# One PSUM pool for attention and MLP, and a fixed order for the first MLP products

## The chip, the cores and the metric

The kernel runs on one core of a Trainium2 chip. The metric is the device time of one execution in microseconds (us): the time before is the median of three runs. Beside them stands one profiled execution, whose trace gives every instruction of the engines: PE (TensorE matmuls; PEld are its weight loads), DVE (VectorE), ACT (ScalarE), POOL (GpSimd) and SP, whose queue issues all DMAs here.

## The reference, cut to what matters

```python
def _attn_ref(q, k, v):                       # 8 batches, 12 heads, 448 positions, head size 64
    scores = scale * np.matmul(q, k.transpose(0, 1, 3, 2)) - np.log(S)
    attn = 1.0 / (1.0 + np.exp(-scores))      # a sigmoid, no row sums
    return np.matmul(attn, v)
x = attn_out.transpose(0, 2, 1, 3).reshape(B * S, H * D)      # 3584 tokens x 768
h = x @ w_in                                  # 768 x 2048 (float64 weights)
r = np.maximum(h, 0.0)
return ((r * r) @ w_out).astype(np.float32)   # 2048 x 768
```

## The kernel before, in words

The first phase is attention, 48 pairs of heads in turn (`step`, L302). For a pair, PE computes four blocks of scores, ACT takes the sigmoid of each into SBUF, and PE multiplies these by v into one PSUM bank, `pav` (L207). DVE copies that bank to `xo` (`put_x`, L219), and a DMA puts it into the scratch array `xd`. The two fp64 weight matrices are converted beside it.

The second phase is the MLP, four groups `g` of two batches. Each matrix product is done as seven products of half-size blocks (numbered 1 to 7, with sums and differences of blocks as operands), and every fp32 operand is split into a high part (`...h`, rounded by a cast) and a low part (`...l`, the remainder by a DVE subtraction), so that each block needs three matmuls: high x high, low x high, high x low. `gemm1` (L367) goes over eight chunks `i` of the hidden units; `run(n, i)` (L391) is product n of chunk i, nine matmuls with 448 columns each. It is called (n, i) below. Products 1, 6, 5 and 3 of a chunk accumulate one after the other in a bank "a", and ACT copies the value between them (`snap`, L387) or takes the ReLU; 7 and 4 go to a bank "b", and 2 to a bank "c". `gemm2` (L431) has three output chunks `e`; each product there is 24 matmuls for each e, and product 3 ends in `put("12", ...)`, an ACT copy out of bank "a" (L462), while product 4 adds to bank "b".

Each bank is a tile of its own from a PSUM pool. Attention has the pool `ps1` (L319): three tiles of two banks for scores, two of one bank for `pav`. The MLP has the pool `ps2` (L354), eight tiles of one bank. The second pool takes the memory of the first, so its first tile waits until the last tile of the first pool has been read.

The order on each engine is that of the code within `manual_schedule` (attention and the first operands of the MLP), and a list scheduler's own elsewhere; it can also slip its instructions between those of the written order. The engines run their queues strictly in order. At the end of attention `x_operands(0)` (L230) loads the attention output of the first two batches back from `xd` and returns eleven pieces: `make` splits a block (cast on ACT, L226; subtraction on DVE, L227), `sub` builds a difference (DVE, L244). The blocks x11, x21, x12, x22 are the operands of products 1, 2, 5 and 3; t1 to t4 are differences (t2 for product 6, t3 for 7, t1 for 5, t4 for 4). Before, the pieces and the weight splits `halve_weights` (L161; ACT cast L165, DVE subtraction L166) stand between the last attention steps, in the counts 1, 3, 3, and the rest after the last `put_x`. `first_44` is the first chunk's weights for products 1, 2, 6, 7, `first_45` those for 5, 3, 4. Weight tiles ("w") have eight buffers, so later weights wait on SP until the matmuls that read an earlier tile have ended. From `gemm2`, at product 3, `ahead` (L505) makes the next group's operands by the same pieces.

Of the kernel before, what the change touches and what calls it, by code (L numbers as in the profile page):

```python
# [41 lines left out]
PLACE = {n: i for i, n in enumerate(PRODUCTS)}  # L42
PH = 4
EARLY, LATE = slice(0, PH), slice(PH, 7)


@with_exitstack
def sigmoid_attention_relu2_mlp(
# [49 lines left out]
    def op1(name, dtype=F32):  # L98
        return sb.tile([P, S], dtype, tag="op1", bufs=N1, name=name)

    def wide(name, dtype=F32):
# [87 lines left out]

    def scores(ps, b, p, x):  # L190
        out = []
        for t in range(NT):
            sc = ps.tile([P, 2, 512], F32, tag="sc", bufs=3, name=f"sc_{b}_{p}_{t}")
            ks = slice(t * KT, (t + 1) * KT)
            for n, (kp, qp) in enumerate(((0, 0), (1, 0), (0, 1))):
                for j in range(2):
                    rows = slice(j * D, (j + 1) * D)
                    nc.tensor.matmul(  # L198
                        sc[:KT, j, :S], x[kp][rows, 1, ks], x[qp][rows, 0], start=(n == 0), stop=(n == 2)
                    )  # L200
            at = op2(f"at_{b}_{p}_{t}")
            nc.scalar.activation(at[:KT], sc[:KT, :, :S], AF.Sigmoid, bias=NEG_LOG_S, scale=SCALE)  # L202
            out.append(at)
        return out

    def attn_v(ps, b, p, at, vt):
        pav = ps.tile([P, 512], F32, tag="pav", bufs=2, name=f"pav_{b}_{p}")  # L207
        for t in range(NT):
            for j in range(2):
                nc.tensor.matmul(  # L210
                    pav[j * D : (j + 1) * D, :S],
                    vt[:KT, t, j * D : (j + 1) * D],
                    at[t][:KT, j],
                    start=(t == 0),
                    stop=(t == NT - 1),
                )
        return pav

    def put_x(b, p, pav):  # L219
        x = op1(f"xo_{b}_{p}")  # L220
        nc.vector.tensor_copy(out=x, in_=pav[:, :S])  # L221
        nc.sync.dma_start(out=xd[b, p], in_=x)

    def split(raw, name, new):
        hi, lo = new(name + "h", F32R), new(name + "l", F32R)
        nc.scalar.copy(out=hi, in_=raw)  # L226
        nc.vector.tensor_sub(out=lo, in0=raw, in1=hi.bitcast(F32))  # L227
        return hi, lo

    def x_operands(g):  # L230


# [14 lines left out]

        def make(product, n):
            (h2, l2), (h1, l1) = (split(r, f"{t}{n}_{g}", new) for r, t, new in zip(raw[n], "xy", (op2, op1)))
            ops[product] = [(h2[:, 0], l2[:, 0]), (h2[:, 1], l2[:, 1]), (h1, l1)]  # L250
# [6 lines left out]
        raw["t1"], raw["t3"], raw["t4"] = raw["12"], raw["11"], raw["21"]  # L257
        return ops, [
            lambda: make(1, "11"),
            lambda: make(2, "21"),  # L260
            lambda: sub("t1", "12", "11"),
            lambda: sub("t2", "22", "t1"),
            lambda: make(6, "t2"),
            lambda: sub("t3", "t2", "11"),
            lambda: make(7, "t3"),
            lambda: make(5, "t1"),
            lambda: make(3, "22"),
            lambda: sub("t4", "21", "t2"),
            lambda: make(4, "t4"),
        ]  # L270

# [29 lines left out]

    def step(ps, n):  # L302

        if n + XA <= last:
            x[n + XA] = load_pair(*pairs[n + XA])
        if n + VA <= last:
            vt[n + VA] = load_v(*pairs[n + VA])
        if n > 0:
            put_x(*pairs[n - 1], pav.pop(n - 1))
        if n + SA <= last:  # L310
            xs[n + SA] = split_pair(*pairs[n + SA], x[n + SA])
        if n < last:
            at[n + 1] = scores(ps, *pairs[n + 1], xs[n + 1])
        pav[n] = attn_v(ps, *pairs[n], at[n], vt[n])
        for k in range(NK):
            if k * NWP // NK == n:
                weights(k)

    with tc.tile_pool(name="ps1", bufs=2, space=PSUM) as ps:  # L319
        with tc.manual_schedule():  # L320
            wp = ps.tile([P, 2, 512], F32, tag="sc", bufs=3, name="warm_ps")
            for i in range(13):
                nc.tensor.matmul(wp[:, 0, :S], warm[:, :P], warm[:, :S], start=True, stop=True)
            x[0] = load_pair(*pairs[0])
            vt[0] = load_v(*pairs[0])
            x[1] = load_pair(*pairs[1])
            f64[0, 0] = load_chunk(*todo[0], 0)
            for n in (1, 2):
                x[n + 1] = load_pair(*pairs[n + 1])
                vt[n] = load_v(*pairs[n])  # L330
            f64[0, 1] = load_chunk(*todo[0], 1)
            for n in range(SA):
                xs[n] = split_pair(*pairs[n], x[n])
            at[0] = scores(ps, *pairs[0], xs[0])
            for n in range(last - 3):
                step(ps, n)
            ops[0], pieces = x_operands(0)
            first = {}
            for n, part, count in ((last - 3, EARLY, 1), (last - 2, LATE, 3), (last - 1, None, 3), (last, None, 0)):
                if part:  # L340
                    first[0, part == LATE] = load_weights(w1[0][:, part], f"first_{n}")
                step(ps, n)
# [12 lines left out]

    def bank(name):
        return ps.tile([P, 512], F32, tag="bank", bufs=8, name=name)[:, :S]

# [8 lines left out]
    def gemm1(g, ops, first):  # L367
# [23 lines left out]
        def run(n, i):  # L391
# [32 lines left out]

        for i in range(NI + 1):
            for n, j in ((1, i), (5, i - 1), (2, i), (6, i), (3, i - 1), (7, i), (4, i - 1)):
                if 0 <= j < NI:
                    run(n, j)
        return blocks

    def gemm2(g, blocks, ahead):  # L431
# [42 lines left out]
        for at, n in enumerate(order):  # L474
# [27 lines left out]
    for g in range(NG):  # L502
        blocks = gemm1(g, ops[g], {} if g else first)

        def ahead():  # L505
            if g + 1 < NG:
                ops[g + 1], pieces = x_operands(g + 1)
                for piece in pieces:
                    piece()

# [33 lines left out]
```

## Time and profile before

| | us |
|---|---|
| median of three runs (lowest, highest) | 1129.76 (1128.61, 1131.07) |
| the profiled execution | 1128.11 |
| its span, first to last instruction | 1126.3 |
| PE busy | 1109.9 (99%) |
| DVE busy | 779.0 (69%) |
| ACT busy | 614.4 (55%) |
| mean granted TensorE clock, as a share of full speed | 0.997 |

Busy time counts overlapping matmuls once. The rows of the trace give a start, a duration, the engine, the source line, the operation, out<-in with buffer and chunk numbers left out (so `w_1l` stands for several chunks, `x` for several blocks), and in brackets how long the engine sat idle before the row and what ended that. Matmuls overlap: the time that one takes in a row of them is the distance of their starts, not the duration shown; the same holds, by a little, for DVE and ACT.

### The profile page before, as it was taken

Reading aid. Unit: us, or ns where it says so; the run is one execution under the profiler, and the core shown is the slowest. Engines: PE = TensorE matmul, PEld = TensorE weight load, DVE = VectorE, ACT = ScalarE, POOL = GpSimd, SP = SyncE. Lnnn points to the kernel's source line nnn. Section 1 sums busy time; section 2 is a strip of 40 time slices with the busy share of each in tenths; the row PEclk is TensorE's granted clock in tenths of the full one; section 3 lists DMA queues with packets and bytes.
Section 4 is the critical chain, followed back from the end, with each engine's and each line's share of the span. In section 5 each row is a group of like instructions: output and inputs, shape, how many; then the busy total and the mean of one; then the engine's idle time right before and its main releaser. Section 6 shows DMA issues by size and latency. Waiting matters only on the chain.

```text
span 1126.3 us, 15056 instructions
## 1 busy us (share of the span) xinstructions
PE 1109.9 (99%) x5965; PEld 903.7 (80%) x5965; DVE 779.0 (69%) x869; ACT 614.4 (55%) x737; POOL 59.6 (5%) x36
## 2 busy tenths in 40 slices
PE   9999999999699999999999999999999999999998
PEld 4555455455499999999999999999999999999998
DVE  6778797877845589773557988454699745559951
ACT  6777787777634366553346466234556534346631
POOL 1122221221000000000000000000000000000000
PEclk9999999999899999999999999999999999999999
DMA  9989999999323333454324445333333652234431
GB/s 306 347 312 351 333 324 338 336 347 335 126 95 118 104 105 122 180 194 136 98 98 134 137 150 197 121 111 133 107 96 125 235 175 99 98 98 141 137 124 62
DMA packets 66503, 202.32 MB, mean 180 GB/s; under 512 B 6784, under 2 KB 33408, under 8 KB 66432
## 3 DMA queue, kind: packets, MB, share of 16 engines
q1 hardware_dynamic: 66432, 201.35, 52.4%
q8 instruction: 47, 0.77, 0.3%
q14 instruction: 24, 0.20, 0.1%
HBM read 157.29 MB, written 44.04 MB: 179 GB/s over the span
## 4 chain that ended last, share of the span: by engine, by line
PE 95%; DMA 2%; DVE 1%; ACT 1%; SPq 0%; issue 0%; ACTq 0%
PE ha L363 21%; PE oa L363 21%; PE pav L210 12%; PE hb L363 10%; PE ob L363 10%; PE sc L198 10%; PE hc L363 5%; PE oc L363 5%; DMA f<-w_in 1%; DMA first_45l<-w 1%; DMA w_1l<-w 0%; ACT at L202 0%; DVE xo L221 0%; DVE w_1l L166 0%; SPq L181 0%
## 5 line engine op out<-in xcount | busy, mean ns | idle before, releaser
L202 ACT ACTIVATE at<-sc 112x896 f32<-112x896 f32 x192 | 160.5, 925 | 69.2 <-PE sc L198 69.2
L166 DVE TENSOR_TENSOR w_1l<-w_1l,w_1h 128x1536 fp32r<-128x1536 f32 x59 | 103.5, 1755 | 87.2 <-ACT w_1h L165 87.2
L210 PE MATMUL pav<-at,v 112*64 112x448 f32 x768 | 154.9, 545 | 0.8 <-DVE xo L221 0.8
L389 ACT COPY s<-ha 128x448 f32<-128x448 f32 x96 | 51.1, 532 | 169.8 <-PE ha L363 147.7
L210 PEld LDWEIGHTS pav<-at,v 112*64 112x64 f32 x768 | 50.8, 136 | 83.7 <-issue 81.3
L165 ACT CAST w_1h<-w_1l 128x1536 fp32r<-128x1536 f32 x59 | 87.4, 1481 | 30.1 <-DMA w_1l<-w 29.7
L198 PE MATMUL sc<-qh 64*112 64x448 f32 x384 | 79.2, 408 | 2.5 <-ACT at L202 2.5
L198 PEld LDWEIGHTS sc<-qh 64*112 64x112 f32 x384 | 33.4, 170 | 51.1 <-issue 23.3
L422 DVE TENSOR_TENSOR g<-hb,s 128x448 f32<-128x448 f32 x32 | 20.0, 624 | 75.4 <-PE hb L363 75.4
L198 PE MATMUL sc<-qh,ql 64*112 64x448 f32 x384 | 70.8, 364 | 0.4 <-DVE ql L187 0.4
L165 ACT CAST w_0h<-w_0l 128x1536 fp32r<-128x1536 f32 x28 | 41.4, 1480 | 54.1 <-DMA w_0l<-w 54.1
L132 POOL TENSOR_TENSOR a<-a,f 128x768 int32<-128x768 int32 x32 | 59.4, 1857 | 212.3 <-DVE a L129 118.7
L198 PE MATMUL sc<-ql,qh 64*112 64x448 f32 x384 | 70.4, 362 | 0.0
L166 DVE TENSOR_TENSOR w_0l<-w_0l,w_0h 128x1536 fp32r<-128x1536 f32 x28 | 49.1, 1755 | 26.7 <-ACT w_0h L165 26.7
L221 DVE COPY xo<-pav 128x448 f32<-128x448 f32 x48 | 29.8, 622 | 50.4 <-PE pav L210 50.4
L165 ACT CAST w_5h<-w_5l 128x1152 fp32r<-128x1152 f32 x31 | 35.9, 1159 | 42.9 <-DMA w_5l<-w 28.2
L166 DVE TENSOR_TENSOR w_5l<-w_5l,w_5h 128x1152 fp32r<-128x1152 f32 x31 | 41.9, 1353 | 20.5 <-ACT w_5h L165 20.0
L187 DVE TENSOR_TENSOR ql<-x,qh 128x896 fp32r<-128x896 f32 x48 | 52.4, 1092 | 1.6
L385 DVE SCALAR_TENSOR_TENSOR g<-g 128x896 f32<-128x896 f32 x48 | 52.2, 1087 | 1.0
L186 DVE CAST qh<-x 128x896 fp32r<-128x896 f32 x48 | 41.0, 854 | 6.2 <-DMA x<-qk 6.2
L198 PEld LDWEIGHTS sc<-ql,qh 64*112 64x112 f32 x384 | 33.6, 171 | 5.5
L464 DVE TENSOR_TENSOR o<-ob,t 128x448 f32<-128x448 f32 x24 | 14.9, 620 | 32.9 <-PE ob L363 26.5
(597 smaller groups left out, 2961.4 us busy)
## 6 DMA issues: line engine op xcount, KB each, us to landing
w_1l<-w SPq DMA_DIRECT2D x59, 768.0 KB, 4.4
x<-qk SPq DMA_DIRECT2D x48, 448.0 KB, 7.3
w_0l<-w SPq DMA_DIRECT2D x28, 768.0 KB, 4.6
w_5l<-w SPq DMA_DIRECT2D x31, 576.0 KB, 4.2
f<-w_in SPq DMA_DIRECT2D x16, 768.0 KB, 6.8
w<-s SPq DMA_DIRECT2D x16, 768.0 KB, 3.8
f<-w_out SPq DMA_DIRECT2D x16, 768.0 KB, 6.3
v<-v SPq DMA_DIRECT2D x48, 224.0 KB, 7.3
```

The costliest lines, as they stand in the source:

```text
L132: nc.gpsimd.tensor_tensor(out=wb, in0=wb, in1=t.bitcast(I32)[:, :, 0], op=ALU.add)
L165: nc.scalar.copy(out=hi, in_=raw)
L166: nc.vector.tensor_sub(out=lo, in0=raw, in1=hi.bitcast(F32))
L186: nc.vector.tensor_copy(out=hi, in_=x)
L187: nc.vector.tensor_sub(out=lo, in0=x, in1=hi.bitcast(F32))
L198: nc.tensor.matmul(sc[:KT, j, :S], x[kp][rows, 1, ks], x[qp][rows, 0], start=(n == 0), stop=(n == 2))
L202: nc.scalar.activation(at[:KT], sc[:KT, :, :S], AF.Sigmoid, bias=NEG_LOG_S, scale=SCALE)
L210: nc.tensor.matmul(pav[j * D : (j + 1) * D, :S], vt[:KT, t, j * D : (j + 1) * D], at[t][:KT, j], start=(t == 0), stop=(t == NT - 1),)
L221: nc.vector.tensor_copy(out=x, in_=pav[:, :S])
L363: nc.tensor.matmul(out, a[:, c], b, start=first and n == 0, stop=last and n == 2, skip_group_check=True)
L385: nc.vector.scalar_tensor_tensor(out=t, in0=t, scalar=0.0, in1=t, op0=ALU.max, op1=ALU.mult)
L389: nc.scalar.copy(out=s, in_=banks["a", i])
```

## The change

There is one PSUM pool for the whole kernel: three tiles of two banks ("two") and two of one bank ("one"). In the MLP, banks "a" and "b" of a chunk are now the two halves of one "two" tile, which is taken at product 1; bank "c" is a "one" tile. The weights of the second chunk's products 1, 2, 6 and 7 (`w1_second`) are loaded within the written order, right behind `w1_late` (formerly `first_45`). The operands of products 1 and 2 are made by DVE alone, cast included: those of 1 behind the last step but two, those of 2 and the difference t1 behind the last step but one, t2 behind the last step. The last `put_x` follows, then the rest of the pieces with two of the weight splits among them. On PE, eleven products of group 0 get a fixed order relative to each other.

```diff
+FIRST_STEPS = ((1, 0), (2, 0), (1, 1), (2, 1), (6, 0), (7, 0), (6, 1), (5, 0), (7, 1), (3, 0), (4, 0))
+    ps = ctx.enter_context(tc.tile_pool(name="ps", bufs=2, space=PSUM))
+    def banks2(name):
+        return ps.tile([P, 2, 512], F32, tag="two", bufs=3, name=name)[:, :, :S]
+    def bank(name):
+        return ps.tile([P, 512], F32, tag="one", bufs=2, name=name)[:, :S]
...
+    def split(raw, name, new, vector=False):
         hi, lo = new(name + "h", F32R), new(name + "l", F32R)
-        nc.scalar.copy(out=hi, in_=raw)
+        if vector:
+            nc.vector.tensor_copy(out=hi, in_=raw)
+        else:
+            nc.scalar.copy(out=hi, in_=raw)
         nc.vector.tensor_sub(out=lo, in0=raw, in1=hi.bitcast(F32))
...
-            for n, part, count in ((last - 3, EARLY, 1), (last - 2, LATE, 3), (last - 1, None, 3), (last, None, 0)):
-                if part:
-                    first[0, part == LATE] = load_weights(w1[0][:, part], f"first_{n}")
-                step(ps, n)
-                if n == last - 2:
-                    halve_weights(first[0, False])
-                if n == last - 1:
-                    halve_weights(first[0, True])
-                for piece in pieces[:count]:
-                    piece()
-                del pieces[:count]
-            put_x(*pairs[last], pav[last])
-            for piece in pieces:
-                piece()
-    ps = ctx.enter_context(tc.tile_pool(name="ps2", bufs=8, space=PSUM))
+        first = {(0, False): load_weights(w1[0][:, EARLY], "w1_first")}
+        step(last - 3)
+        first[0, True] = load_weights(w1[0][:, LATE], "w1_late")
+        first[1, False] = load_weights(w1[1][:, EARLY], "w1_second")
+        step(last - 2)
+        pieces_of(1, vector=True)
+        halve_weights(first[0, False])
+        step(last - 1)
+        pieces_of(2, "t1", vector=True)
+        step(last)
+        pieces_of("t2")
+        put_x(*pairs[last], pav[last])
+        pieces_of(6)
+        halve_weights(first[1, False])
+        pieces_of("t3", 7)
+        halve_weights(first[0, True])
+        pieces_of(5, 3, "t4", 4)
...
-            if n in (1, 7, 2):
-                banks[k, i] = bank(f"h{k}_{g}_{i}")
+            if n == 1:
+                ab = banks2(f"h_{g}_{i}")
+                banks["a", i], banks["b", i] = ab[:, 0], ab[:, 1]
+            elif n == 2:
+                banks["c", i] = bank(f"hc_{g}_{i}")
...
+        if g == 0:
+            with tc.manual_schedule(engines={mybir.EngineType.PE}):
+                for n, i in FIRST_STEPS:
+                    run(n, i)
+            steps = [x for x in steps if x not in FIRST_STEPS]
...
-                if n in (1, 7, 2):
-                    banks[k, e] = bank(f"o{k}_{g}_{e}")
+                if n == 1:
+                    ab = banks2(f"o_{g}_{e}")
+                    banks["a", e], banks["b", e] = ab[:, 0], ab[:, 1]
+                elif n == 2:
+                    banks["c", e] = bank(f"oc_{g}_{e}")
```

The order on PE where the MLP begins: the first matmul of each piece of a product, before. In a name such as `ha_0_1` the numbers are the group and the chunk; `w1_0_1_1h` are the weights of chunk 1.

```order
L363 MATMUL ha_0_0_3264<-x11_0h_3073,first_44h_3009 128x448
...
L363 MATMUL hc_0_0_3276<-x21_0h_3138,first_44h_3009 128x448
...
L363 MATMUL hb_0_0_3299<-xt3_0h_3210,first_44h_3009 128x448
...
L363 MATMUL ha_0_1_3314<-x11_0h_3073,w1_0_1_1h_3309 128x448
...
L363 MATMUL ha_0_0_3264<-xt2_0h_3200,first_44h_3009 128x448
...
L363 MATMUL ha_0_1_3314<-x11_0l_3074,w1_0_1_1h_3309 128x448
```

The same place on PE of the changed kernel; the fifth to seventh rows are the first three matmuls of (1, 2).

```order
L378 MATMUL h_0_0_3267<-x11_0h_3131,w1_firsth_3009 128x448
...
L378 MATMUL hc_0_0_3279<-x21_0h_3189,w1_firsth_3009 128x448
...
L378 MATMUL h_0_1_3291<-x11_0h_3131,w1_secondh_3076 128x448
...
L378 MATMUL hc_0_1_3303<-x21_0h_3189,w1_secondh_3076 128x448
...
L378 MATMUL h_0_2_3396<-x11_0h_3131,w1_0_2_1h_3391 128x448
L378 MATMUL h_0_2_3396<-x11_0l_3132,w1_0_2_1h_3391 128x448
L378 MATMUL h_0_2_3396<-x11_0h_3131,w1_0_2_1l_3392 128x448
...
L378 MATMUL h_0_0_3267<-xt2_0h_3216,w1_firsth_3009 128x448
```

Product (1, 2), which is not among the eleven, stands between the fourth and the fifth of them, and needs the weights of chunk 2, high and low.

DVE behind the copy that the last `pav` product but one waits for, before (`xo_7_5` is the last copy of attention):

```order
L221 COPY xo_7_3_3150<-pav_7_3_3127 128x448
L166 TENSOR_TENSOR first_45l_3082<-first_45l_3082,first_45h_3081 128x1152
L227 TENSOR_TENSOR xt2_0l_3201<-xt_0_3007,xt2_0h_3200 128x896
L227 TENSOR_TENSOR yt2_0l_3205<-yt_0_3008,yt2_0h_3204 128x448
L244 TENSOR_TENSOR x11_0_2991<-xt_0_3007,x11_0_2991 128x896
L244 TENSOR_TENSOR y11_0_2992<-yt_0_3008,y11_0_2992 128x448
L166 TENSOR_TENSOR w1_0_1_1l_3310<-w1_0_1_1l_3310,w1_0_1_1h_3309 128x1536
L227 TENSOR_TENSOR xt3_0l_3211<-x11_0_2991,xt3_0h_3210 128x896
L227 TENSOR_TENSOR yt3_0l_3215<-y11_0_2992,yt3_0h_3214 128x448
L221 COPY xo_7_4_3218<-pav_7_4_3189 128x448
L221 COPY xo_7_5_3230<-pav_7_5_3221 128x448
```

DVE of the changed kernel from its last copy of attention; the second half of each pair (y, 448 wide) is left out from the third row on.

```order
L231 COPY xo_7_5_3213<-pav_7_5_3202 128x448
L240 TENSOR_TENSOR xt2_0l_3217<-xt_0_3007,xt2_0h_3216 128x896
L240 TENSOR_TENSOR yt2_0l_3221<-yt_0_3008,yt2_0h_3220 128x448
L176 TENSOR_TENSOR w1_secondl_3077<-w1_secondl_3077,w1_secondh_3076 128x1536
L258 TENSOR_TENSOR x11_0_2991<-xt_0_3007,x11_0_2991 128x896
...
L240 TENSOR_TENSOR xt3_0l_3229<-x11_0_2991,xt3_0h_3228 128x896
...
L176 TENSOR_TENSOR w1_latel_3074<-w1_latel_3074,w1_lateh_3073 128x1152
L240 TENSOR_TENSOR xt1_0l_3239<-x12_0_2995,xt1_0h_3238 128x896
...
L240 TENSOR_TENSOR x22_0l_3247<-x22_0_2999,x22_0h_3246 128x896
...
L258 TENSOR_TENSOR x21_0_3003<-x21_0_3003,xt_0_3007 128x896
...
L176 TENSOR_TENSOR w1_0_2_1l_3392<-w1_0_2_1l_3392,w1_0_2_1h_3391 128x1536
```

The copies have moved ahead of the MLP's operands, and the low part of chunk 2's weights is the last of what stands here.

PE in `gemm2` of group 0, the first matmuls of product 4 for e = 0, 1, 2 with the engines that they wait for, before:

```order
L363 MATMUL ob_0_0_4363<-o4_0_0h_4552,w2_0_4_0h_4571 128x448 [waits Activation_49]
L363 MATMUL ob_0_0_4363<-o4_0_0l_4553,w2_0_4_0h_4571 128x448
...
L363 MATMUL ob_0_1_4388<-o4_0_0h_4552,w2_0_4_0h_4571 128x448
L363 MATMUL ob_0_1_4388<-o4_0_0l_4553,w2_0_4_0h_4571 128x448
...
L363 MATMUL ob_0_2_4413<-o4_0_0h_4552,w2_0_4_0h_4571 128x448
```

And of the changed kernel, where bank "b" of chunk e is a half of the tile `o_0_e`:

```order
L378 MATMUL o_0_0_4021<-o4_0_0h_4540,w2_0_4_0h_4559 128x448 [waits Activation_49]
L378 MATMUL o_0_0_4021<-o4_0_0l_4541,w2_0_4_0h_4559 128x448
...
L378 MATMUL o_0_1_4048<-o4_0_0h_4540,w2_0_4_0h_4559 128x448 [waits Activation_49]
L378 MATMUL o_0_1_4048<-o4_0_0l_4541,w2_0_4_0h_4559 128x448
...
L378 MATMUL o_0_2_4075<-o4_0_0h_4540,w2_0_4_0h_4559 128x448 [waits Activation_49]
```

The matmuls for e = 1 and e = 2 now wait for ACT, which they did not before; for e = 0 the wait is there in both.

## Rows read from the trace of the kernel before

**Rows 1.** PE's waits: who for whom, total us, times, longest us.

```profile
PE ha L363 <- DVE xo L221: 8.2, 1, 8.2
```

**Rows 2.** Timeline of PE, last attention product and first MLP products.

```profile
290.14 3.23 PE L210 MATMUL pav<-at,v 112*64 112x448 f32 x16 [0.78 <-DVE xo L221]
...
301.53 0.74 PE L363 MATMUL ha<-x_0h,first_44h 128*128 128x448 f32 x1 [8.16 <-DVE xo L221]
...
304.96 0.37 PE L363 MATMUL hc<-x_0h,first_44h 128*128 128x448 f32 x1
...
306.82 0.37 PE L363 MATMUL hb<-xt_0h,first_44h 128*128 128x448 f32 x1
...
308.68 0.37 PE L363 MATMUL ha<-x_0h,w_1h 128*128 128x448 f32 x1
```

**Rows 3.** Windows: from:to, length, busy us (count) by engine, granted clock, DMA.

```profile
300.00:305.00 5.00, 3.47 (x10) 3.11 (x11) 5.00 (x8) 2.38 (x4) 0.00 (x0) 0.52 0.25 92
305.00:310.00 5.00, 5.00 (x26) 4.55 (x25) 4.82 (x6) 1.84 (x3) 0.00 (x0) 1.00 0.00 0
```

**Rows 4.** Timeline of DVE where attention ends.

```profile
289.47 0.61 DVE L221 COPY xo<-pav 128x448 f32<-128x448 f32 x1
290.01 1.34 DVE L166 TENSOR_TENSOR first_45l<-first_45l,first_45h 128x1152 fp32r<-128x1152 f32 x1
291.27 1.08 DVE L227 TENSOR_TENSOR xt_0l<-xt,xt_0h 128x896 fp32r<-128x896 f32 x1
292.27 0.61 DVE L227 TENSOR_TENSOR yt_0l<-yt,yt_0h 128x448 fp32r<-128x448 f32 x1
292.81 1.08 DVE L244 TENSOR_TENSOR x<-xt,x 128x896 f32<-128x896 f32 x1
...
297.12 1.76 DVE L166 TENSOR_TENSOR w_1l<-w_1l,w_1h 128x1536 fp32r<-128x1536 f32 x1 [2.69 <-ACT w_1h L165]
298.79 1.08 DVE L227 TENSOR_TENSOR xt_0l<-x,xt_0h 128x896 fp32r<-128x896 f32 x1
...
300.33 1.15 DVE L221 COPY xo<-pav 128x448 f32<-128x448 f32 x2
```

**Rows 5.** Timeline of ACT in the same stretch and behind it.

```profile
295.61 1.47 ACT L165 CAST w_1h<-w_1l 128x1536 fp32r<-128x1536 f32 x1 [5.16 <-DMA w_1l<-w]
296.99 0.93 ACT L226 CAST xt_0h<-x 128x896 fp32r<-128x896 f32 x1
297.83 0.56 ACT L226 CAST yt_0h<-y 128x448 fp32r<-128x448 f32 x1
...
315.10 1.15 ACT L165 CAST w_5h<-w_5l 128x1152 fp32r<-128x1152 f32 x1
```

**Rows 6.** Timeline of SP's DMA queue.

```profile
278.94 11.49 SPq L222 DMA_DIRECT2D xd<-xo  x2
290.52 0.88 SPq L158 DMA_DIRECT2D w_1l<-w  x2
...
311.39 0.32 SPq L158 DMA_DIRECT2D w_5l<-w  x1
```

**Rows 7.** The costliest group of DVE casts of this shape (page, part 5).

```profile
L186 DVE CAST qh<-x 128x896 fp32r<-128x896 f32 x48 | 41.0, 854 | 6.2 <-DMA x<-qk 6.2
```

**Rows 8.** Timelines: PE's first matmul of product 4, groups 0, 1, 2.

```profile
494.82 0.36 PE L363 MATMUL ob<-o_0h,w_0h 128*128 128x448 f32 x1
...
699.22 0.36 PE L363 MATMUL ob<-o_0h,w_0h 128*128 128x448 f32 x1
...
903.72 0.36 PE L363 MATMUL ob<-o_0h,w_0h 128*128 128x448 f32 x1
```

**Rows 9.** Timelines: ACT's three copies out of bank "a", groups 0, 1, 2.

```profile
495.93 1.58 ACT L462 COPY o<-oa 128x448 f32<-128x448 f32 x3
...
700.07 1.58 ACT L462 COPY o<-oa 128x448 f32<-128x448 f32 x3
...
904.99 1.58 ACT L462 COPY o<-oa 128x448 f32<-128x448 f32 x3
```

More of the change, by code (lines that the diff above doesn't have):

```diff
@@ L188, in split_pair, with scores @@
         return hi, lo
-    def scores(ps, b, p, x):
+    def scores(b, p, x):
         out = []
         for t in range(NT):
-            sc = ps.tile([P, 2, 512], F32, tag="sc", bufs=3, name=f"sc_{b}_{p}_{t}")
+            sc = banks2(f"sc_{b}_{p}_{t}")
             ks = slice(t * KT, (t + 1) * KT)
@@ L198, in scores, with attn_v @@
                     nc.tensor.matmul(
-                        sc[:KT, j, :S], x[kp][rows, 1, ks], x[qp][rows, 0], start=(n == 0), stop=(n == 2)
+                        sc[:KT, j], x[kp][rows, 1, ks], x[qp][rows, 0], start=(n == 0), stop=(n == 2)
                     )
             at = op2(f"at_{b}_{p}_{t}")
-            nc.scalar.activation(at[:KT], sc[:KT, :, :S], AF.Sigmoid, bias=NEG_LOG_S, scale=SCALE)
+            nc.scalar.activation(at[:KT], sc[:KT], AF.Sigmoid, bias=NEG_LOG_S, scale=SCALE)
             out.append(at)
         return out
-    def attn_v(ps, b, p, at, vt):
-        pav = ps.tile([P, 512], F32, tag="pav", bufs=2, name=f"pav_{b}_{p}")
+    def attn_v(b, p, at, vt):
+        pav = bank(f"pav_{b}_{p}")
         for t in range(NT):
@@ L210, in attn_v @@
                 nc.tensor.matmul(
-                    pav[j * D : (j + 1) * D, :S],
+                    pav[j * D : (j + 1) * D],
                     vt[:KT, t, j * D : (j + 1) * D],
@@ L220, in put_x @@
         x = op1(f"xo_{b}_{p}")
-        nc.vector.tensor_copy(out=x, in_=pav[:, :S])
+        nc.vector.tensor_copy(out=x, in_=pav)
         nc.sync.dma_start(out=xd[b, p], in_=x)
-    def split(raw, name, new):
+    def split(raw, name, new, vector=False):
         hi, lo = new(name + "h", F32R), new(name + "l", F32R)
-        nc.scalar.copy(out=hi, in_=raw)
+        if vector:
+            nc.vector.tensor_copy(out=hi, in_=raw)
+        else:
+            nc.scalar.copy(out=hi, in_=raw)
         nc.vector.tensor_sub(out=lo, in0=raw, in1=hi.bitcast(F32))
@@ L246, in x_operands, with make @@
         ops = {}
-        def make(product, n):
-            (h2, l2), (h1, l1) = (split(r, f"{t}{n}_{g}", new) for r, t, new in zip(raw[n], "xy", (op2, op1)))
+        def make(product, n, vector=False):
+            (h2, l2), (h1, l1) = (split(r, f"{t}{n}_{g}", new, vector) for r, t, new in zip(raw[n], "xy", (op2, op1)))
             ops[product] = [(h2[:, 0], l2[:, 0]), (h2[:, 1], l2[:, 1]), (h1, l1)]
@@ L300, in sigmoid_attention_relu2_mlp, with step @@
     NK = 3 * len(todo) + 1
-    def step(ps, n):
+    def step(n):
         if n + XA <= last:
@@ L312, in step @@
         if n < last:
-            at[n + 1] = scores(ps, *pairs[n + 1], xs[n + 1])
-        pav[n] = attn_v(ps, *pairs[n], at[n], vt[n])
+            at[n + 1] = scores(*pairs[n + 1], xs[n + 1])
+        pav[n] = attn_v(*pairs[n], at[n], vt[n])
         for k in range(NK):
@@ L354, in sigmoid_attention_relu2_mlp, with pieces_of @@
-    ps = ctx.enter_context(tc.tile_pool(name="ps2", bufs=8, space=PSUM))
-    def bank(name):
-        return ps.tile([P, 512], F32, tag="bank", bufs=8, name=name)[:, :S]
+    with tc.manual_schedule():
+        wp = banks2("warm_ps")
+        for i in range(13):
+            nc.tensor.matmul(wp[:, 0], warm[:, :P], warm[:, :S], start=True, stop=True)
+        x[0] = load_pair(*pairs[0])
+        vt[0] = load_v(*pairs[0])
+        x[1] = load_pair(*pairs[1])
+        f64[0, 0] = load_chunk(*todo[0], 0)
+        for n in (1, 2):
+            x[n + 1] = load_pair(*pairs[n + 1])
+            vt[n] = load_v(*pairs[n])
+        f64[0, 1] = load_chunk(*todo[0], 1)
+        for n in range(SA):
+            xs[n] = split_pair(*pairs[n], x[n])
+        at[0] = scores(*pairs[0], xs[0])
+        for n in range(last - 3):
+            step(n)
+        ops[0], pieces = x_operands(0)
+        first = {(0, False): load_weights(w1[0][:, EARLY], "w1_first")}
+        def pieces_of(*names, vector=False):
+            for name in names:
+                pieces[name](vector)
+        step(last - 3)
[14 more added lines that the diff above has]
+        pieces_of(5, 3, "t4", 4)
@@ L423, in run @@
                 squares("21", i)
[L425 to L428, printed above, removed]
+        steps = [
+            (n, j)
+            for i in range(NI + 1)
+            for n, j in ((1, i), (5, i - 1), (2, i), (6, i), (3, i - 1), (7, i), (4, i - 1))
+            if 0 <= j < NI
+        ]
+        if g == 0:
[3 more added lines that the diff above has]
+            steps = [x for x in steps if x not in FIRST_STEPS]
+        for n, i in steps:
+            run(n, i)
         return blocks
@@ L507, in ahead @@
                 ops[g + 1], pieces = x_operands(g + 1)
-                for piece in pieces:
-                    piece()
+                for piece in pieces.values():
+                    piece(False)
         gemm2(g, blocks, ahead)
```

46 lines of the change are left out of this document (13 added, 33 removed).

## The prediction

> **What bounds the kernel now.** I read the waits of TensorE first, since the page has PE busy for 99% of the span. The longest single wait by far is that of the first MLP matmul for DVE's last copies of attention [rows 1]. The timeline shows the place: the last attention product starts at 290.14 after 0.78 us of idle time for an earlier such copy, runs 3.23 us, and then PE is idle for 8.16 us, to 301.53 [rows 2]. The reader should see who ends the wait: two copies that start at 300.33 and take 1.15 us [rows 4], so to 301.48, and PE goes on 0.05 us later. That 0.05 is my price of a hand-over from here on. The copies were not late for want of data, since the product that they read had ended by 293.37; DVE worked through its written order, and one of its entries waited for a weight load (2.69 us idle at 297.12, whose cast on ACT had waited 5.16 us for the DMA) [rows 4, 5]. Behind the wait PE is slow: the first product's nine matmuls take from 301.53 to 304.96, 3.43 us, the third's from 306.82 to 308.68, 1.86 us, or 0.207 for one [rows 2]; the granted clock is 0.52 of full speed in 300 to 305 and 1.00 behind [rows 3], so the first nine ran at 1.2 GHz and the later ones at 2.4. The price of the whole transition is 0.78 + 8.16 + (3.43 - 1.86) = 10.5 us. Everywhere else in the MLP PE is gapless, so whatever makes it wait there is added to the time in full.
>
> **The change part by part.**
>
> *The pool wait goes.* A score tile is free long before 293, so the first MLP product no longer waits for the last copies. Their earlier place also frees the `pav` bank in time: the 0.78 goes. Attention then ends at 290.14 - 0.78 + 3.23 = 292.59, and PE goes straight on, if the operands of products 1 and 2 are there.
>
> *Products 1 and 2 by DVE.* Four casts come onto DVE. A 128x896 cast is 0.85 in the mean [rows 7]; the 448 wide one is not in the trace, at least 0, at most 0.85; I take 0.6, near the 448 wide subtraction (0.61). From starts in rows 4: a 448 copy 0.54, a pair of subtractions (896 and 448) 1.00 + 0.54 = 1.54, a 1152 split 1.26, a 1536 split 1.67. Before, three pairs stand between the first weights' split and the copy at 289.47, so that split was done by 289.47 - 4.62 = 284.85. Now come a copy, a split of x21 with its casts (1.54 + 1.45), t1 (1.54), a copy, t2 (1.54): 7.15 in all, to 292.0. The last copy has to wait for PE until 292.6 anyhow, so the casts cost nothing. That cover is 0.6 us; past it every microsecond delays the chain below by as much.
>
> *Four products run, then PE waits again.* (1,0), (2,0), (1,1) and (2,1) take 4 x 1.86 = 7.44, to 300.0. The next on PE is (1,2), which is not one of the eleven; its first two matmuls need the high part of chunk 2's weights, the third the low part. On DVE that low part is the last of what follows the last copy: 0.54 (copy) + 6 x 1.54 (t2 split, t3, t3 split, t1 split, x22 split, t4) + 1.67 + 1.26 + 1.76 (the three weight splits) = 14.47. DVE also waits for ACT's cast of t3: it starts 1.08 into the pair and takes 0.93 [rows 5], so 2.01 + 0.1 against 1.54, some 0.6. From 292.64 that is 307.7, and the third matmul can go at 307.8. The high part comes earlier: t3 is there at 292.64 + 0.54 + 1.54 + 1.67 + 1.08 = 297.5, and ACT then has three pairs of casts (0.84 + 0.56 each), the late weights (1.15) and this cast (1.47) [rows 5], to 304.3. So PE is idle from 300.0 to 307.8 but for two matmuls, 7.4 us, in place of 8.9: the wait has moved behind four products more than it has shrunk.
>
> *What that is worth.* I count matmuls done. The clock fell in the pause before; I take it that it falls in this one too, and that nine matmuls are slow again: 38 are done at 307.8 and 47 at 311.2. Before, 9 were done at 304.96 and 9 + 6.24 / 0.207 = 39 at 311.2. The gain is 8 x 0.207 = 1.6 us. From above: if the clock stays up, 1.57 more. From below: the load `w1_0_1_5` may start only when the first weights' last reader, now (7,0), has ended. Before it took from the issue at 311.39 to the end of the cast at 316.25 and 1.34 for the split, 6.2 us [rows 4 to 6]. Now 27 + 3 matmuls lie between (7,0) and the third of (5,1), 30 x 0.207 = 6.2; I take a wait of 0.3 (with a load as slow as the 5.1 us at 290.52, 1.4 more). The net gain is 1.3.
>
> *The loads.* The second chunk's weights went to DMA at 290.52, behind two copies that SP had waited 11.49 us to send [rows 6]; now they stand ahead of these, so at about 279, and are needed at 293. The third chunk's stand behind the last copies, so about 293.3; with the 5.1 us from issue to cast shown for both of 290.52 they are there by 298.4, needed at about 302.8. Neither costs anything.
>
> *Banks "a" and "b" in one tile.* In `gemm2`, product 4 adds to bank "b" while ACT still has to copy product 3's result out of "a". The order shows that the first matmul of product 4 now waits for ACT for e = 1 and 2, where before it did not: the tile is guarded as a whole. For e = 0 I read its old wait as the operand's and its new one as the later of operand and copy. In the trace product 4 starts at 494.82, 699.22 and 903.72 [rows 8], the three copies at 495.93, 700.07 and 904.99, each 1.58 / 3 = 0.53 [rows 9]. With the copy of e = 0 to wait for, PE stands 1.64, 1.38 and 1.80 us, with 0.05 each 4.97 in all. The copies of e = 1 and 2 end 1.05 later, behind one and two pieces of 24 matmuls (4.9 us each), and cost nothing. The fourth group makes no operands for a next one and its copies come promptly. ACT's queue ahead of the copies is the casts of the next group's operands, which are the same in both orders, and the transition shifts PE and them alike; so I take the whole 4.97. Bounds: 0, if the copies came as soon as product 3 ends, and 3 x 1.80 + 0.15 = 5.6.
>
> A rule of the Trainium skill speaks against this term. Its page PSUM — Partial Sum Buffer, section "PSUM bank collisions raise a hardware error", says that accesses have to be kept apart by bank (and quadrant), not more widely; the two halves are different banks. By that rule alone the sum would be without the 4.97. No run here shows the collision itself, but the wait stands in the program's order, whether the chip needs it or not.
>
> *The eleven products' order* otherwise costs nothing: a product is the same nine matmuls wherever it stands.
>
> **The sum.** 1128.11 (profiled execution) - 1.3 + 4.97 = 1131.8. The median of the runs lies 1.65 above that execution, so 1133.4.
>
> **Rivals.**
>
> *The four products bridge the gap* (faster). If what PE needs next were ready within 7.4 us of the end of attention, all 10.5 us would go, and with the 5.0 in `gemm2` the time would be 1129.76 - 10.5 + 5.0 = 1124.3. For it: DVE idled 2.69 us in this stretch [rows 4]. Against it: the chain is 14.5 us of plain DVE work.
>
> *The two halves cost no wait* (no change): the mechanism is a copy that is done before product 4 wants the bank, or the page's rule. 1129.76 - 1.3 = 1128.5. Against it: three groups out of three show the copy late by over 1.3 us.
>
> *The clock stays up in the new pause*, since two matmuls lie inside: 1133.4 - 1.57 = 1131.9. Against it: it had fallen in the one pause of this length that the trace has.
>
> *The transition gains nothing*: (5,1) waits 1.4 us more for its weights, or the casts overrun their cover. 1129.76 + 5.0 = 1134.8 and somewhat above.
>
> **Chances.** The forecast 0.60 (its own range 1132.2 to 1135.0), clock up 0.13, no gain 0.11, no wait in the halves 0.09, bridge 0.07. A measurement of this kernel tells 0.2%, 2.3 us, from no change; so slower begins at 1132.0. Slower: 0.57 of the forecast, the 0.11, and 0.05 of the clock's: 0.73. Same: the rest of these and the 0.09: 0.20. Faster 0.07. The range from 1130.8 to 1135.9 leaves out the bridge, most of the unwaited halves and a little above.
>
> **What would show it.** PE: the first MLP matmul right behind the last `pav`, about 292.6; a gap of some 7 us ahead of and in (1,2), ended by ACT's cast and DVE's split of chunk 2's weights; nine slow matmuls behind it; then a PE wait for ACT's copy of line 489 in three groups, 1.4 to 1.8 us each. It is wrong if (1,2) starts without a wait, if these three waits are missing, or if other waits of over 0.5 us on the halves of a tile appear in `gemm1`.

## The result and the profile after

The changed kernel took 1133.55 us (median of 11 runs, 1131.24 to 1135.40) against 1128.61 for the kernel before, timed beside it: a ratio of 1.0044, 95% interval 1.0029 to 1.0058, so some 5 us slower. The prediction was 1133.4, that is 3.6 us above the 1129.76 that it started from. The profiled execution took 1133.89 us, its span is 1132.1.

The waits of PE over the whole span of the changed kernel (engine and line, what ended the wait: us in total, times, the longest):

```profile
PE h L378 <- ACT w_1h L175: 3.9, 1, 3.9
PE o L378 <- ACT o L489: 3.7, 3, 1.6
...
PE h L378 <- DVE w_1l L176: 2.6, 1, 2.6
...
PE h L378 <- DVE g L431: 0.4, 1, 0.4
```

The 8.2 us of [rows 1] are gone. A wait of 3.9 and 2.6 us for the third chunk's weights stands in their place, three waits for ACT's copies are new, and so is one for an add of DVE (`g`, L431). PE's timeline shows the places (start, us, instruction, [idle before it <- releaser]):

```profile
292.73 0.47 PE L378 MATMUL h<-x_0h,w_firsth 128*128 128x448 f32 x1
...
300.00 0.37 PE L378 MATMUL hc<-y_0h,w_secondl 128*128 128x448 f32 x1
304.27 0.74 PE L378 MATMUL h<-x_0h,w_1h 128*128 128x448 f32 x1 [3.90 <-ACT w_1h L175]
304.81 0.57 PE L378 MATMUL h<-x_0l,w_1h 128*128 128x448 f32 x1
307.98 0.74 PE L378 MATMUL h<-x_0h,w_1l 128*128 128x448 f32 x1 [2.59 <-DVE w_1l L176]
308.51 0.57 PE L378 MATMUL h<-x_0h,w_1h 128*128 128x448 f32 x1
...
312.25 0.48 PE L378 MATMUL h<-xt_0l,w_firsth 128*128 128x448 f32 x1
312.57 0.36 PE L378 MATMUL h<-xt_0h,w_firstl 128*128 128x448 f32 x1
...
495.79 0.47 PE L378 MATMUL o<-o_0h,w_0h 128*128 128x448 f32 x1 [0.84 <-ACT o L489]
...
701.74 0.47 PE L378 MATMUL o<-o_0h,w_0h 128*128 128x448 f32 x1 [1.27 <-ACT o L489]
...
908.05 0.47 PE L378 MATMUL o<-o_0h,w_0h 128*128 128x448 f32 x1 [1.64 <-ACT o L489]
...
1002.46 0.47 PE L378 MATMUL h<-x_3h,w_5h 128*128 128x448 f32 x1 [0.42 <-DVE g L431]
```

The MLP starts at 292.73, right behind attention, where it was 301.53 [rows 2]. Four products later PE stops, does two matmuls, stops again, and from 308.51 to 312.25 a matmul takes 0.374 us. The windows say the same (us, busy us and instructions of each engine, granted clock, DMA):

```profile
295.00:300.00 5.00, 5.00 (x26) 4.55 (x25) 4.47 (x6) 2.23 (x3) 0.00 (x0) 1.00 0.47 157
300.00:305.00 5.00, 1.09 (x4) 0.50 (x2) 5.00 (x7) 4.22 (x6) 0.00 (x0) 0.73 0.00 0
305.00:310.00 5.00, 2.41 (x7) 1.83 (x6) 5.00 (x7) 2.27 (x4) 0.00 (x0) 0.50 0.02 3
310.00:315.00 5.00, 5.00 (x20) 4.33 (x19) 1.62 (x2) 0.53 (x1) 0.00 (x0) 0.75 0.00 0
```

A clock of 0.50 is the level of 1.2 GHz, as in [rows 3]. DVE is busy all through the pause. Its timeline has the last attention copy and the end of the chain to the third chunk's weights:

```profile
292.85 0.63 DVE L231 COPY xo<-pav 128x448 f32<-128x448 f32 x1 [0.68 <-PE pav L220]
...
306.17 1.75 DVE L176 TENSOR_TENSOR w_1l<-w_1l,w_1h 128x1536 fp32r<-128x1536 f32 x1
```

An account of PE's lost time: for each of the 4032 MLP matmuls of both traces I took by how much the interval between two starts exceeds the usual one (0.203 us, or 0.207 in stretches that the last section speaks of; I call this usual interval the pace). A wait comes out some 0.15 us longer this way than in PE's list, which counts from the shown end of the matmul before: 1.43 for the 1.27 at 701.74. Transition and `gemm1` of group 0: before 0.78 + 8.24 + 1.60 = 10.6, now 10.06, a gain of 0.55. `gemm2` of groups 0 to 2: 1.07 + 1.52 + 1.89 = 4.5 more. `gemm1` of group 3: 1.37 against 0.06, 1.3 more. Together 5.25; the spans differ by 5.8, of which 0.3 is a difference in pace and 0.2 lies in attention, from its start on. The executions of one kernel differ by up to 1%, and the pace alone is worth 11 us in one of the traces below, so the experiments are read by this account first and by their medians second. The ratio given with each run is against the kernel before, timed beside it. That kernel's own median there was 1130.75 (first four runs), 1130.83 (fifth to eighth) and 1129.70 (last two), against the 1128.61 beside the changed kernel, which was not timed again: a difference between a run's median and the changed kernel's 1133.55 is uncertain by some 2 us.

### The profile page after: what moved, and what is told of

Same layout as the page of the kernel before. It is cut to its first block, busy times and chain, and to the rows that moved or that the text cites. A ratio compares the mean times of both kernels' runs of the same rounds, so it can differ in the third digit from the quotient of the medians.

```text
span 1132.1 us, 15052 instructions
## 1 busy us (share of the span) xinstructions
PE 1113.6 (98%) x5965; PEld 903.8 (80%) x5965; DVE 782.7 (69%) x873; ACT 612.8 (54%) x733; POOL 59.8 (5%) x36
## 4 chain that ended last, share of the span: by engine, by line
PE 91%; DVE 3%; DMA 3%; ACT 2%; issue 1%; SPq 1%; ACTq 0%; DVEq 0%
PE h L378 30%; PE o L378 27%; PE pav L220 13%; PE sc L208 11%; PE oc L378 5%; PE hc L378 5%; DMA f<-w_in 1%; DMA w_0l<-w 1%; DMA w_1l<-w 1%; DVE w_1l L176 0%; DMA y<-xd 0%; DVE y L258 0%; ACT at L212 0%; ACT w_0h L175 0%; DVE x L258 0%
## 5 line engine op out<-in xcount | busy, mean ns | idle before, releaser
L404 ACT COPY s<-h 128x448 f32<-128x448 f32 x96 | 50.9, 533 | 164.9 <-PE h L378 141.2
L440 DVE TENSOR_TENSOR g<-h,s 128x448 f32<-128x448 f32 x32 | 20.0, 624 | 69.8 <-PE h L378 69.7
L378 PE MATMUL o<-o_0h,w_0h 128*128 128x448 f32 x144 | 52.3, 368 | 3.7 <-ACT o L489 3.7
L378 PE MATMUL o<-o_2h,w_1l 128*128 128x448 f32 x144 | 52.7, 366 | 0.0
L378 PE MATMUL o<-o_3l,w_1h 128*128 128x448 f32 x144 | 52.7, 366 | 0.0
```

The costliest lines, as they stand in the source:

```text
L378: nc.tensor.matmul(out, a[:, c], b, start=first and n == 0, stop=last and n == 2, skip_group_check=True)
L404: nc.scalar.copy(out=s, in_=banks["a", i])
L440: nc.vector.tensor_add(out=tile_of("21", i), in0=out, in1=snaps[2, i])
```

## The experiments

My theory was that two things decide: entries of DVE and ACT that stand in their queues ahead of what PE needs next, and the tile that guards banks "a" and "b" as one. Its rivals stand with each run.

**The pairing alone.** Before, with the halves of one tile in the second pool:

```diff
...
-            if n in (1, 7, 2):
-                banks[k, e] = bank(f"o{k}_{g}_{e}")
+            if n == 1:
+                ab = banks2(f"o_{g}_{e}")
+                banks["a", e], banks["b", e] = ab[:, 0], ab[:, 1]
+            elif n == 2:
+                banks["c", e] = bank(f"oc_{g}_{e}")
```

> The kernel before with one part of the change alone: in the MLP, banks a and b of one chunk are the two halves of one tile, in before's second pool (3 two-bank tiles, 2 one-bank tiles). The transition is as in before. Theory (the halves cost waits): in the changed kernel PE stood about 1.0, 1.4 and 1.8 us ahead of product 4 of gemm2 in the first three groups, and some 1.3 us more went in gemm1 of the last group; so this kernel is 4 to 5.5 us slower than before, and its trace shows a PE wait for ACT's copies of product 3's result, three times, that before does not have. Rival 1 (the copy is late only because the transition moved ACT's work): no such waits, within 1 us of before. Rival 2 (PE is slower for other reasons, a drift of the matmul pitch between two executions): no waits and yet some 2 us slower.

1134.01 us, ratio 1.0036 (1.0012 to 1.0059). The waits have both, the old one and the new:

```profile
PE h L366 <- DVE xo L221: 8.1, 1, 8.1
PE o L366 <- ACT o L468: 4.0, 3, 1.4
```

By the account `gemm2` loses 1.56, 1.53 and 1.65. So the pairing makes the three waits, with the old transition too. The second pool also has fewer tiles here than before's eight, but product 4 takes no new tile, so it is not their number that it waits for. `gemm1` of group 3 lost nothing (0.11): that part of the expectation missed.

**Fewer casts ahead of the copies.** The changed kernel, with the next group's operands made in two parts:

```diff
-            if n == 3:
-                ahead()
+            if n in (3, 4):
+                ahead(n)    # 3: operands of products 1 and 2; 4: the others
...
```

> The changed kernel, with one edit in gemm2: of the next group's operands only those of products 1 and 2 are made ahead of product 3, the others behind product 3, so that ACT comes to its copies of product 3's result with fewer casts in front. The tile pairing stays. Theory (it is the late copy, not the pairing by itself, that PE waits for): the three PE waits of 1.0, 1.4 and 1.8 us go, no new ones at the next group's start; 4.2 us faster than the changed kernel, some 0.5 us slower than before to 0.5 faster. Rival 1 (the pairing costs whatever ACT does, for instance because reading one bank holds up writes to its neighbour): no more than 1 us faster than the changed kernel. Rival 2 (the operands of products 6, 7 and on come late for the next group): new waits of 1 us or more in gemm1 of groups 1 to 3 take the gain back.

1125.64 us, ratio 0.998 (0.9949 to 1.001): no difference from before is clear of the noise. The profiled execution, at 1137.42, is the slowest of the twelve, by its pace (last section). No wait for ACT's copies is left in the list, and `gemm2` loses nothing in any group. The pairing costs only where the copy is late.

**Product (1,2) as the twelfth:**

```diff
-(6, 1), (5, 0), (7, 1), (3, 0), (4, 0))
+(6, 1), (5, 0), (7, 1), (3, 0), (4, 0), (1, 2))
```

> The changed kernel, with product (1,2) as the twelfth of the fixed order, so that it can no longer come between the fourth and the fifth. Theory of the prediction (PE waits for chunk 2's weights): with seven more products ahead of (1,2), 13 us, its weights are there in time, PE waits less than 2 us, and the kernel is 6 to 9 us faster than the changed one. Rival (the rest of the transition is as late: product (6,0) writes bank a, which ACT has first to copy, and this copy stands on ACT behind all casts of the transition): PE does four products and waits about as long as in the changed kernel, 6 to 8 us, now ahead of (6,0) and for ACT; within 1.5 us of the changed kernel. I think the rival likelier.

1134.17 us, 1.0026 (1.0006 to 1.0047), as the rival had it. PE's wait, and then ACT's timeline:

```profile
PE h L378 <- ACT s L404: 7.3, 1, 7.3
```

```profile
292.19 1.47 ACT L175 CAST w_secondh<-w_secondl 128x1536 fp32r<-128x1536 f32 x1
...
301.96 1.47 ACT L175 CAST w_1h<-w_1l 128x1536 fp32r<-128x1536 f32 x1
304.96 0.94 ACT L239 CAST xt_0h<-x 128x896 fp32r<-128x896 f32 x1 [1.53 <-DVE x L258]
305.80 0.56 ACT L239 CAST yt_0h<-y 128x448 fp32r<-128x448 f32 x1
306.27 0.96 ACT L404 COPY s<-h 128x448 f32<-128x448 f32 x2
```

L404 copies bank "a" out after product 1; product (6,0) needs it. Product (1,0), begun at 291.94, had ended by 294, but its copy stands behind every cast of the transition, to 306.27.

**The pause filled.** 18 matmuls that nobody reads, into a bank that product 7 later clears:

```diff
+            if (g, n, i) == (0, 1, 2):
+                for _ in range(18):
+                    nc.tensor.matmul(banks["b", i], first[0, False][0][:, 0, :P], ops[1][0][0], start=True, stop=True)
```

> The changed kernel with 18 matmuls more, whose result nobody reads: one a little earlier, 17 right ahead of (1,2), where PE waits 3.9 us for the high part of chunk 2's weights. 17 x 0.207 = 3.5 us, so they should delay nothing. What it tells: whether the slow stretch behind the pause (matmuls from 307.98 to 312.4 at 0.374 us instead of 0.207) comes from the pause. Theory (the clock falls since PE stands idle): the second part of the pause, 2.6 us, alone remains, the granted clock stays at 1.00 behind it or falls for less long, and the kernel is 1.5 to 2.2 us faster than the changed one. Rival 1 (the second part is enough, or the clock falls for another reason): same time as the changed kernel within 0.7 us. Rival 2 (the fill delays the product): up to 1 us slower.

1130.98 us, 1.0007 (0.9984 to 1.003). The median is 2.6 below the changed kernel's, which would suit the theory, but the trace is the first rival's: 13 matmuls are slow again, and with the fill's own 3.7 us counted as lost, `gemm1` of group 0 loses 10.5, where it was 10.06. (Group 3 lost nothing in this execution, 1.3 less; the rest of the median's gain I can't place. The two ratios against before put the gain at 4 us, known to some 3.) PE was busy until 304, then stood 3.0 us, and the clock fell:

```profile
300.00:305.00 5.00, 4.41 (x21) 3.42 (x19) 5.00 (x7) 4.02 (x6) 0.00 (x0) 1.00 0.01 3
305.00:310.00 5.00, 2.24 (x6) 2.02 (x7) 5.00 (x7) 2.27 (x4) 0.00 (x0) 0.62 0.00 0
310.00:315.00 5.00, 5.00 (x18) 4.31 (x18) 1.40 (x2) 0.53 (x1) 0.00 (x0) 0.70 0.00 0
```

So the second part of the pause was enough. The eighth run, below, fills it too.

**The order woven for all engines.** Each split, copy and add of DVE and ACT is written where PE comes to need it. PE's fixed order changes with it: nine products in place of eleven, with (6,1) ahead of (7,0).

```diff
...
-        pieces_of("t2")
+        halve_weights(first[1, False])
         put_x(*pairs[last], pav[last])
+    def begin(run, post):    # post: the copies and adds behind a product
+        run(1, 0)
+        pieces_of("t2", 6)
+        post(1, 0)
+        run(2, 0)
+        pieces_of("t3", 7)
+        run(1, 1)
...
-            with tc.manual_schedule(engines={mybir.EngineType.PE}):
+            with tc.manual_schedule():
+                begin(run, post)
```

> The changed kernel, with the transition written as one order for all engines: VectorE's and ScalarE's entries (operands, weight splits, copies out of bank a, adds) stand among the first products in the order in which PE comes to need them; the split of the second chunk's weights goes ahead of the last attention copy, the adds behind. PE's order: (1,0), (2,0), (1,1), (2,1), (6,0), (6,1), (7,0), (7,1), (5,0), then the scheduler's. One pool and the paired halves stay. Theory (no data of these nine products is late, only the place of its work in the queues of ACT and DVE): the pause of 4.1 + 3.0 us and the 2 to 3 us of slow matmuls behind it go, at most 2 us of small waits come, so 7 to 9 us faster than the changed kernel, about 1125; the three waits of 1 to 1.8 us ahead of product 4 of gemm2 stay. Rival 1 (DVE has 14.5 us of work behind the last copy and stays the bound): the same idle time in smaller pieces, under 3 us gained. Rival 2 (weights of chunk 2 or the second half of chunk 1 land late): a new pause of 2 us or more at (1,2) or (5,1).

1126.03 us, 0.9969 (0.9947 to 0.9991). By the account the first group's `gemm1` loses 2.17 in place of 10.06; what PE still waits for in the MLP is

```profile
PE o L397 <- ACT o L511: 4.6, 3, 1.9
...
PE h L397 <- DVE g L453: 0.8, 2, 0.4
PE hc L397 <- DVE w_1l L176: 0.5, 1, 0.5
PE h L397 <- DVE w_1l L176: 0.3, 1, 0.3
```

The same work on DVE and ACT, placed otherwise, leaves 2.17 us: the pause was a matter of place in the queues, not of too much work on DVE.

**Both edits**, woven order and split casts:

> The edits of the second and the fifth run together: transition woven for all engines, and the next group's operands behind product 1 and 2's made after product 3. Theory (the two terms add): the transition gives 7 to 9 us and the three waits 4 to 4.5 us, 11 to 13 us faster than the changed kernel and 6 to 9 us faster than before, about 1120 to 1122. Rival 1 (the gains overlap, for instance because an earlier start of group 0 meets later weights): under 9 us faster than the changed kernel. Rival 2 (no gain over before, the executions differ by more): within 2 us of before.

1120.01 us, 0.9948 (0.9914 to 0.9981), the lowest median. It lies 10.8 us below the 1130.83 of before beside it, but the ratio stands for 6 us only (2 to 10): eight of the twelve executions took 1118 to 1122 us and four 1129 to 1132. All that PE waits for in its MLP is

```profile
PE hc L397 <- DVE w_1l L176: 0.8, 1, 0.8
PE h L397 <- DVE g L453: 0.6, 1, 0.6
PE h L397 <- DVE w_5l L176: 0.2, 1, 0.2
```

**Two pools again.** The changed kernel with before's `ps1` and `ps2` (eight separate banks), the rest kept:

```diff
...
-                ab = banks2(f"o_{g}_{e}")
-                banks["a", e], banks["b", e] = ab[:, 0], ab[:, 1]
+                banks[k, e] = one(f"o{k}_{g}_{e}")    # from ps2, for n in (1, 7, 2)
```

> The changed kernel without its first part: attention and MLP have the two PSUM pools of before, eight separate banks in the MLP; VectorE's casts, the second chunk's weights and the eleven products in fixed order stay. Theory (with VectorE's new order the last attention copy comes only some 0.7 us behind the end of attention, so the pool change buys little, and the paired halves cost 4.5 us): PE waits 0.5 to 1.2 us for that copy ahead of the first product, then again some 7 us behind four products, and none in gemm2; 3 to 5 us faster than the changed kernel, within 1.5 us of before. Rival (the one pool is what moves PE's start): the first product waits 3 us or more for the copies, and the kernel is no faster than the changed one.

1129.78 us, 1.0004 (0.9983 to 1.0025), as the theory had it. The pause behind four products stands here ahead of (6,0), for ACT's copy, as in the third run:

```profile
PE ha L383 <- ACT s L409: 6.5, 1, 6.5
...
PE ha L383 <- DVE xo L231: 0.7, 1, 0.7
```

**Both parts of the pause filled**, 14 such matmuls more between the second and third matmul of (1,2):

> The changed kernel with 32 matmuls more whose result nobody reads: the 18 of the fourth run ahead of (1,2), and 14 (14 x 0.207 = 2.9 us) between its second and third matmul, where PE waited 3.0 us more. Theory (the clock falls because PE stands, and in the fourth run the second part of the pause was enough for it): granted clock 1.00 throughout the transition, no matmul at 0.374, and 2 to 2.7 us faster than the changed kernel. Rival (the clock falls at this place whatever PE does): a dozen slow matmuls as before, within 0.7 us of the changed kernel, or slower, since the fill itself then takes longer than the pause.

1129.04 us, 1.0005 (0.9988 to 1.0022), 4.5 below the changed kernel's median. No matmul at 0.374 is left:

```profile
300.00:305.00 5.00, 4.66 (x23) 4.00 (x22) 5.00 (x8) 3.48 (x5) 0.00 (x0) 1.00 0.00 0
305.00:310.00 5.00, 4.83 (x24) 4.14 (x23) 4.96 (x7) 1.81 (x4) 0.00 (x0) 1.00 0.00 0
310.00:315.00 5.00, 5.00 (x26) 4.43 (x25) 0.44 (x1) 0.57 (x2) 0.00 (x0) 1.00 0.20 42
```

Only PE's standing had cost the clock. With the fill's own 6.5 us counted as lost, `gemm1` of group 0 loses 8.3, so 1.8 us come back, a little under the 2 to 2.7 expected; of the rest of the median's gain 1.3 is group 3, where this execution lost nothing, and the rest is within the noise of the medians.

**A late add, with shared and with separate banks.** Both have in `gemm1` of group 3

```diff
                 snap(4, i)
+                if g == NG - 1:
+                    for _ in range(3):
+                        nc.vector.tensor_copy(out=snaps[4, i], in_=snaps[4, i])
                 nc.vector.tensor_add(out=tile_of("22", i), in0=banks["b", i], in1=snaps[4, i])
```

> The kernel of the first run (before with the halves of one tile in the MLP), with more work on VectorE: in gemm1 of the last group, product 5's copy of bank a is copied onto itself three times (3 x 0.5 us) ahead of the add that reads it and bank b, so this add comes 1.6 us later in each of the eight chunks. Question: the changed kernel lost 1.3 us in this stretch, where one wait of PE (0.42 us) ended with that add. Theory (product 3 writes bank a, the other half of the tile that the add still reads): PE waits for the add or behind it in most chunks, 3 to 5 us in all in this stretch, and the kernel is slower than the first run's by as much. Rival (PE waited for the late weights, and the add only ended at the same moment): no more waits here than in the tenth run, which has the same extra work and separate banks.

> The kernel before, with the same extra work of VectorE as in the ninth run: three copies of 0.5 us ahead of product 5's add, in each chunk of gemm1 of the last group. Banks a and b are separate tiles here. Theory (only the shared tile makes PE wait for that add): under 0.6 us of new waits of PE in this stretch, the time within 1 us of before. Rival (VectorE at 69% busy has no room for 12 us more, and the weight splits come late): waits of 3 us or more here too, as in the ninth run.

Shared: 1137.78 us, 1.0071 (1.0043 to 1.0099); separate: 1129.07, 1.0002 (0.9984 to 1.002). By the account this stretch loses 1.89 us with the shared tile and 0.07 with separate banks. The windows, shared and then separate:

```profile
925.00:1035.00 110.00, 109.26 (x533) 98.75 (x532) 65.78 (x83) 46.91 (x58) 0.00 (x0) 1.00 0.34 109
```

```profile
925.00:1035.00 110.00, 110.00 (x543) 101.61 (x543) 73.87 (x91) 49.05 (x62) 0.00 (x0) 1.00 0.35 111
```

The sign is the theory's, the size under the 3 to 5 us expected: the add mostly still ended in time. The ninth run's list has one wait here and puts it down to a copy of ACT, but that copy ended at 1006.76, when PE had already begun to load this product's weights (1006.73). PE goes on 0.15 us behind the add's end, here and at 941.32 and 980.13:

```profile
1006.00 0.62 DVE L422 TENSOR_TENSOR g<-h,s 128x448 f32<-128x448 f32 x1
```

```profile
1006.76 0.44 PE L366 MATMUL h<-x_3h,w_5h 128*128 128x448 f32 x1 [0.63 <-ACT s L392]
```

Of the 1.89 us some 0.9 fell at this one place, where weights had landed late too (ACT had stood 1.78 us for them at 1001.12), and the tenth run had no such landing in this stretch. So the pair of runs shows that the shared tile makes PE wait for the add, but not what the extra work alone costs.

## Why the prediction came out

Its time was met to 0.2 us by luck, because two errors of 2 us cancelled; its mechanism held, but it named half of the cause in one place and missed a term.

*The pool wait and DVE's casts.* Right: the MLP began at 292.73 (predicted 292.6), the last copy waited 0.68 us for PE (cover 0.6). The casts took 0.62 and 0.39, not 0.85 and 0.6. But the prediction did not tell the pool's part from that of DVE's order. The seventh run does: with that order, two pools cost a wait of 0.7, so the one pool was worth 0.7 and not the 8.2 of [rows 1].

*The wait behind four products.* Right to 0.2 us: 304.27 and 307.98 for the first and third matmul of (1,2), predicted 304.3 and 307.8. Incomplete in its cause: the prediction saw only DVE's chain to the weights. Product (6,0) was as late, by ACT's copy (the third run), so that a later place for (1,2) alone does not help; the fifth run shows that neither had to come so late.

*Its worth.* Mis-sized: a gain of 1.3 was expected, 0.55 came. From 307.98 on some twelve matmuls were slow, not nine, besides the two in the pause. The rival in which the clock stays up fell; the eighth run shows what it would have taken. The wait of (5,1) was 0.14 (predicted 0.3).

*The halves of one tile.* The mechanism held (first and second run); predicted 4.97, measured 4.5. Groups 1 and 2 came as read from [rows 8, 9] (1.43 and 1.79 against 1.43 and 1.85). In group 0 the copy started at 495.22, 0.4 us after PE's turn, where [rows 8, 9] had 1.1: ACT came 0.7 earlier than before, PE at the same time, while I had shifted both alike. The first of the three copies in this row ends at 495.75, and PE goes on at 495.79:

```profile
495.22 1.58 ACT L489 COPY o<-o 128x448 f32<-128x448 f32 x3
```

*A term that was missing.* I put a price on false waits in `gemm2` alone; for `gemm1` I only named them as a sign of being wrong, from 0.5 us on. There product 3 writes bank "a" while DVE's add of product 5 may still read "b". In group 3 the weights landed late, the add stood behind their split on DVE, and PE went on 0.05 us behind the add's end:

```profile
949.75 0.62 DVE L431 TENSOR_TENSOR g<-h,s 128x448 f32<-128x448 f32 x1
...
1000.12 1.76 DVE L176 TENSOR_TENSOR w_1l<-w_1l,w_1h 128x1536 fp32r<-128x1536 f32 x1 [4.64 <-ACT w_1h L175]
1001.79 0.62 DVE L431 TENSOR_TENSOR g<-h,s 128x448 f32<-128x448 f32 x1
```

```profile
950.43 0.47 PE L378 MATMUL h<-x_3h,w_5h 128*128 128x448 f32 x1
```

```profile
998.61 1.48 ACT L175 CAST w_1h<-w_1l 128x1536 fp32r<-128x1536 f32 x1 [1.46 <-DMA w_1l<-w]
```

This came three times: PE went on at 950.43, 976.23 and 1002.46 and lost 0.3, 0.3 and 0.7 us there by the account, nearly all of the 1.3; PE's list shows the last alone, with 0.42, just under my sign. The loss follows the late landing. In `gemm1` of groups 1 to 3, the changed kernel and the second, third, fifth, sixth and eighth run have ten such places, each with PE 0.05 us behind the add. There ACT had waited between 1.02 and 1.67 us for the weights' load, and PE's loss grows with that wait, from 0.25 to 0.89; where ACT waited 0.86 us or less, PE lost under 0.1. It does not come in each execution: in group 3 the first, fourth and eighth run lost 0.1. Why the loads land late is open.

*The sum.* The profiled execution came to 1133.89, not 1131.8: 0.75 from the smaller gain, 1.3 from the missing term, -0.5 from the halves, 0.5 from the pace and attention. The 1.65 that I added for the median was not there: this execution lay 0.34 above its median. The kernel before, timed beside the changed one, was 1.15 below the median that I started from, so the step from before to after was 4.9 us, where I had 3.6.

The Trainium skill's page PSUM — Partial Sum Buffer, section "PSUM bank collisions raise a hardware error", gave no ground on the chip for these waits, and the tenth run agrees: with separate banks and the same late add, PE loses 0.07 us. The wait is the program's.

## What to carry to other kernels

A tile of two banks is guarded as one: put into it only what is written and read at the same time, or see to it that the reader of one half is never late. A fixed order for one engine is none until the queues of the engines that feed it are written in the same order; ask of each first product which copy, cast and add it needs, and what stands ahead of these. When a wait goes, the next thing late is found by the same question.

## What the hardware showed besides

PE has two paces at a granted clock of 1.00. In one stretch of `gemm1` and `gemm2` without a wait, the kernel before and the second run show these windows, in this order:

```profile
530.00:690.00 160.00, 160.00 (x791) 148.15 (x790) 117.59 (x114) 83.30 (x97) 0.00 (x0) 1.00 0.41 135
```

```profile
530.00:690.00 160.00, 160.00 (x776) 145.40 (x775) 116.62 (x113) 80.75 (x94) 0.00 (x0) 1.00 0.39 129
```

That is 0.2027 and 0.2067 us from start to start. The slower pace held for a stretch of some 98 us in the profiled execution of before (305 to 403) and of 585 us in the second run's (worth 1.9 and 11 us). Its cause is open.

How long the clock stays low behind the same pause differs: 9 slow matmuls in the trace of before, 16 in the first run's, 12 or 13 in the tenth's. And a short stop can do it: in the third run PE stood 1.76 us at 704.05, and the clock fell for eight matmuls, while the 1.64 us at 908.05 of the changed kernel and the third run's own 1.68 us at 912.00 left it up:

```profile
700.00:705.00 5.00, 3.24 (x17) 2.65 (x16) 4.29 (x8) 3.44 (x9) 0.00 (x0) 1.00 0.49 166
705.00:710.00 5.00, 5.00 (x19) 4.50 (x17) 1.76 (x1) 1.43 (x2) 0.00 (x0) 0.66 0.88 290
```
